# Loading an output projection with six consecutive rows per partition, and reordering attention's result to match

## The chip, the cores and the metric

The kernel runs on one core of one Trainium2 chip. The metric is the device time of one execution in microseconds (us); lower is better. The core has a matrix engine (TensorE, PE in the profile; its weight loads are PEld), a vector engine (VectorE, DVE), a scalar engine (ScalarE, ACT), GpSimd (POOL), a queue engine (SyncE, SP) and 16 DMA engines that move data from HBM into SBUF, the on-chip memory of 128 partitions. TensorE writes its results into PSUM.

## The reference

One token of 640 values passes through two kinds of layer, each applied twice: attention over a cached window (A), then a small mixer with an MLP (B). The weights and caches are the same both times.

```python
x = A_x
x = x + _A_ref(_layernorm(x), A_k_cache, A_v_cache, A_wq, A_wo)
x = x + _B_ref(_layernorm(x), B_w1, B_w2, B_w3, B_w4)
x = x + _A_ref(_layernorm(x), A_k_cache, A_v_cache, A_wq, A_wo)
x = x + _B_ref(_layernorm(x), B_w1, B_w2, B_w3, B_w4)

# _A_ref: 32 heads of 192, the last 4096 rows of each head's cache
q = (x @ wq).reshape(32, 192)
scores = q . k * 192 ** -0.5        # per head, over 4096 rows
o = softmax(scores) @ v             # per head, 192 values
return o.reshape(32 * 192) @ wo     # wo is 6144 x 640
```

All inputs are bfloat16. For a single token the shifts in `_B_ref` bring only zeros, so its `w1` and `w2` do not reach the result, and the kernel loads `w3` and `w4` alone.

## The kernel before, in words

**Groups.** The 32 heads are handled in 8 groups of 4 (`G = 4`). One `attention` call walks the groups in `order`: 0 to 7 in the first attention, 7 to 0 in the second. A head's K window is one tile of 128 partitions x 6144 bfloat16 values (1536 KB), 32 consecutive cache rows to a partition, so 12,288 consecutive bytes of HBM to each partition; V is the same. These tiles live in 15 `slots`, given out and taken back through the deque `free`. At the turn of the two attentions group 7 keeps its transposed K and its V in SBUF (`keep_T`, `keep`), and the `wo` tiles of groups 6 and 7 stay too.

**Loads.** All large loads are issued by SyncE, in the order of the list `plan` makes: for each group the K heads of the next group and the V heads of this one in turn, after the second V head the group's part of `wo` (L117), and at the end of an attention the mixer's `w3` and `w4` (`load_w34`). A load is issued when the program reaches it (`ahead`) and its slot is free. `plan` fixes 14 loads of `wo` in all: 8 in the first attention, 6 in the second (groups 5 to 0).

**One group.** `keys` transposes K in 32x32 blocks on VectorE (L300, two instructions a head); `kmm` multiplies with the queries (L340), which `qproj` has brought into the block form `Q8` (L288). `soft_a`, `soft_b` and `soft_c` make the softmax (L356 to L401). `pv_rows` multiplies with V (L447), gathering four heads in `O_ps`: afterwards 32 partitions belong to one head each by a pattern that the 0/1 matrix `ho` selects.

**The end of a group, `evac_rows`.** ScalarE (L478) and VectorE (L479) scale and add the two halves of `O_ps` into `O_sb`, 128 partitions x 192. Four products with `O_sb` as weights and columns of `ho` (L482, L484, L486, L488), all in float32, sum over partitions and turn the result: `OT_ps` has 128 partitions x 6, one column for each 128 consecutive entries of the group's 768 outputs. A copy casts it to `osb` (L491).

**The output projection, `outproj`.** The group's 768 rows of `wo` are in `wo_g`, 128 partitions x 6 x 640. Row `t * 128 + p` lies in partition `p` at index `t` ("(t p) n -> p t n" on L117), so that a partition takes six separate rows of 1280 bytes. 30 products of one column (L498) add `wo_g[:, t, :]` times column `t` of `osb` into `y_ps`.

The last group of an attention (`gz`) is treated apart: two of its heads go through `pv_rows` and `evac_rows`, the other two through `pv_cols` and `evac_cols`, which makes `osb` in the order of 128 consecutive entries directly.

The tile `half` (128 x 3072 bfloat16) holds the softmax's `E` and `ET`, `O_lo`, `O_sb` and one of two `PT` tiles during attention, and a part of `w4` during the mixer (L135, L136).

Of the kernel before, what the change touches and what calls it, by code (L numbers as in the profile page):

```python
# [8 lines left out]
BF16 = mybir.dt.bfloat16  # L9
F32 = mybir.dt.float32  # L10
U32 = mybir.dt.uint32
ACTF = mybir.ActivationFunctionType
ALU = mybir.AluOpType
AX = mybir.AxisListType
PSUM = bass.MemoryType.PSUM

P = 128
G = 4
# [7 lines left out]
def kernel(  # L26
# [64 lines left out]
    O_lo = half[:, 2 * NC_S:2 * NC_S + 2 * Dh].bitcast(F32)  # L91
    PT_h = half[:, 2 * NC_S + 4 * Dh:2 * NC_S + 4 * Dh + 4 * G * J]
    O_sb = half[:, 2 * NC_S + 2 * Dh:2 * NC_S + 4 * Dh].bitcast(F32)

    def slot():
        return free.popleft()
# [13 lines left out]

    wo_t = {}

    def load_wo(g):
        if g in wo_t:
            return
        t = wop.tile([P, NOC, D], BF16, name="wo_g")
        nc.sync.dma_start(t[:], A_wo[g * GD:(g + 1) * GD, :].rearrange("(t p) n -> p t n", p=P))  # L117
        wo_t[g] = t

    NKA = FREE // F  # L120
# [66 lines left out]
    for x in range(2):  # L187
# [6 lines left out]
    nc.vector.tensor_reduce(  # L194
        out=ho8[:], in_=ident[:].rearrange("p (tl i e) -> p tl i e", tl=4, e=2)[:, :, 0:G], op=ALU.add, axis=AX.X)
    nc.vector.tensor_reduce(out=ho[:], in_=ho8[:].rearrange("p tl i -> p i tl"), op=ALU.add, axis=AX.X)
    hs = const.tile([P, G], F32, name="hs")
    hs8 = const.tile([P, 8], F32, name="hs8")
    nc.vector.tensor_reduce(
# [72 lines left out]
    def qproj(g, xn_bf):  # L272
        qT_ps = psm.tile([P, NOC], F32, tag="psm", name="qT_ps")
        for tl in range(NOC):
            t = g * NOC + tl
            for kc in range(ND):
                nc.tensor.matmul(  # L277
                    qT_ps[:, tl:tl + 1], lhsT=wq_t[kc][:, t * P:(t + 1) * P], rhs=xn_bf[:, kc:kc + 1],
                    start=(kc == 0), stop=(kc == ND - 1))
        Xq = sm.tile([P, NOC, 4], BF16, name="Xq")  # L280
        nc.vector.tensor_tensor(  # L281
            out=Xq[:], in0=qT_ps[:, :].unsqueeze(2).broadcast_to([P, NOC, 4]),
            in1=maskq[:, :].unsqueeze(1).broadcast_to([P, NOC, 4]), op=ALU.mult)
        Qrep_ps = psm.tile([P, NOC * 4], F32, tag="psm", name="Qrep_ps")
        nc.tensor.matmul(Qrep_ps[:], lhsT=Lb[:].rearrange("p a i -> p (a i)"), rhs=Xq[:].rearrange("p t b -> p (t b)"), start=True, stop=True)
        Q8 = sm.tile([P, 2, 2 * NCOL, 8], BF16, name="Q8", tag=f"Q8_{nq[0] % 2}", bufs=1)
        nq[0] += 1
        nc.vector.tensor_tensor(  # L288
            out=Q8[:],
            in0=Qrep_ps[:, :].rearrange("p (x c) -> p x c", x=2).unsqueeze(3).broadcast_to([P, 2, 2 * NCOL, 8]),  # L290
            in1=blk8[:].unsqueeze(2).broadcast_to([P, 2, 2 * NCOL, 8]), op=ALU.mult)
        Q_t[g] = Q8

# [182 lines left out]
    def evac_rows(g):  # L476
        m01, O_ps = sx[g]["m01"], O_t[g]
        nc.scalar.activation(O_lo, O_ps[:, Dh:2 * Dh], ACTF.Identity, scale=m01[:, 1:2])  # L478
        nc.vector.scalar_tensor_tensor(  # L479
            out=O_sb, in0=O_ps[:, 0:Dh], scalar=m01[:, 0:1], in1=O_lo, op0=ALU.mult, op1=ALU.add)  # L480
        OT_ps = psm.tile([P, 2, 3], F32, tag="psm", name="OT_ps")
        nc.tensor.matmul(OT_ps[:, :, 0], lhsT=O_sb[:, 0:P], rhs=ho[:, 0:4:2], start=True, stop=True,  # L482
                         skip_group_check=True)
        nc.tensor.matmul(OT_ps[:, :, 2], lhsT=O_sb[:, TB:Dh], rhs=ho[:, 1:4:2], start=True, stop=True,  # L484
                         skip_group_check=True)
        nc.tensor.matmul(OT_ps[0:TB, :, 1], lhsT=O_sb[:, P:Dh], rhs=ho[:, 0:4:2], start=True, stop=True,  # L486
                         tile_position=(0, 0), skip_group_check=True)
        nc.tensor.matmul(OT_ps[TB:P, :, 1], lhsT=O_sb[:, 0:TB], rhs=ho[:, 1:4:2], start=True, stop=True,  # L488
                         tile_position=(0, TB), skip_group_check=True)
        osb = sm.tile([P, 2, 3], BF16, name="osb")  # L490
        nc.vector.tensor_copy(osb[:], OT_ps[:])  # L491
        osb_t[g] = osb

    def outproj(g, pr, y_ps, first, last):
        osb = osb_t[g]
# [9 lines left out]
    def attention(order, xT_cur, xT_new, keep, loads):  # L505
        n_loaded = [0]

        def need(upto):
            while n_loaded[0] < min(upto, len(loads)):
                what = loads[n_loaded[0]]  # L510
                n_loaded[0] += 1
                if what[0] == "wo":
                    load_wo(what[1])
                elif what[0] == "w34":
                    load_w34()
                else:
                    load(*what)

        where = {what: n for n, what in enumerate(loads)}
        ahead = lambda *what: need(where.get(what, -1) + 1)  # L520

        def keys(h, whole=True):
            if h not in T_t and h not in half_t:
                ahead("K", h)
                trans_begin(h)
            if whole and h in half_t:
                trans_end(h)

        tot_ps, rstd = ln_stats(xT_cur)
        xn_bf = sm.tile([P, ND], BF16, name="xn_bf")  # L530
        ln_apply(xn_bf, xT_cur, tot_ps, rstd)
        y_ps = psY.tile([P, ND], F32, name="y_ps")
        g0, g1 = order[0], order[1]
        warm = g0 * G in T_t
        qproj(g0, xn_bf)
        for i in range(G):
            keys(g0 * G + i)
            kmm(g0, i)
            if not warm and i == 0:
                qproj(g1, xn_bf)  # L540
        if warm:
            need(G + 1)
        soft_a(g0)
        soft_b(g0)
        if warm:
            keys(g1 * G, whole=False)
            qproj(g1, xn_bf)
        soft_c(g0, g1 * G)
        kept = lambda g, i: ("V", g * G + i) in keep
        for n, g in enumerate(order[:-1]):  # L550
            nxt = order[n + 1]
            ahead_h = order[n + 2] * G if n + 2 < len(order) else None
            for i in range(G):
                keys(nxt * G + i)
                kmm(nxt, i)
                if i == G - 1:
                    soft_a(nxt)
                    soft_b(nxt)
                    if ahead_h is not None:
                        keys(ahead_h, whole=False)  # L560
                ahead("V", g * G + i)
                if i == 1 and ahead_h is not None:
                    qproj(order[n + 2], xn_bf)
                if i == 0:
                    norm_rows(g)
                pv_rows(g, i, kept(g, i))
            ahead("wo", g)
            soft_c(nxt, ahead_h)
            evac_rows(g)
            if ahead_h is not None:  # L570
                outproj(g, 0, y_ps, n == 0, False)
                outproj(g, 1, y_ps, False, False)
        gz = order[-1]
        for i in range(2):
            ahead("V", gz * G + i)
            pv_rows(gz, i, kept(gz, i), n_heads=2)
        outproj(g, 0, y_ps, False, False)
        outproj(g, 1, y_ps, False, False)
        ahead("wo", gz)
        norm_rows(gz)  # L580
        ahead("V", gz * G + 2)
        pv_cols(gz, 2, kept(gz, 2))
        evac_rows(gz)
        outproj(gz, 0, y_ps, False, False)
        ahead("V", gz * G + 3)
        pv_cols(gz, 3, kept(gz, 3))
        evac_cols(gz, 1)
        outproj(gz, 1, y_ps, False, True)
        Oc_t.clear()
        need(len(loads))  # L590
        nc.vector.tensor_tensor(out=xT_new[:], in0=xT_cur[:], in1=y_ps[:], op=ALU.add)
# [35 lines left out]
    def plan(order, have):  # L627
        loads = [("K", order[0] * G + i) for i in range(G)]
        for n, g in enumerate(order):
            for i in range(G):  # L630
                if n + 1 < len(order):
                    loads.append(("K", order[n + 1] * G + i))
                loads.append(("V", g * G + i))
                if i == 1:
                    loads.append(("wo", g))
        loads.append(("w34",))
        return [w for w in loads if w not in have]
# [4 lines left out]
    keep_T = {gl * G + i for i in range(G)}  # L642
    keep = {("V", gl * G + i) for i in range(G)}
    x1 = const.tile([P, ND], F32, name="x1")
    attention(first, xT, x1, keep, plan(first, set()))
    x2 = const.tile([P, ND], F32, name="x2")
    mixer(x1, x2)
# [1 line left out]
        del wo_t[g]  # L649
    have = keep | {("K", h) for h in keep_T} | {("wo", g) for g in wo_t}  # L650
    keep_T = set()
    x3 = const.tile([P, ND], F32, name="x3")
    attention(second, x2, x3, set(), plan(second, have))
    x4 = const.tile([P, ND], F32, name="x4")
# [37 lines left out]
```

## Time and profile before

| | |
|---|---|
| time, median of 3 runs | 540.31 us (539.6 to 540.43) |
| the profiled execution's own time | 539.87 us |
| its span, first to last instruction | 537.6 us |
| moved by DMA | 218.76 MB in 33,830 packets, mean 407 GB/s |
| busy share of the span | PE 59%, PEld 29%, DVE 51%, ACT 7% |
| granted TensorE clock, mean | 0.681 of full speed |

The profile is one execution seen by the hardware profiler. A line of a group reads: source line, engine, operation, output <- inputs, shapes, count | busy us, mean ns of one | idle time of the engine just ahead of it and what ended that. The slice rows cut the span into 40 pieces of 13.44 us. The chain is followed back from the last instruction to what released each step. L12 is line 12 of the kernel.

### The profile page before, as it was taken

To read this page: it belongs to the slowest core of one execution; us is meant where nothing else is said; L and a number is where in the kernel's file an instruction comes from. 1 tells how busy PE (TensorE), PEld (TensorE's weight loads), DVE (VectorE), ACT (ScalarE), POOL (GpSimd) and SP (SyncE) were. 2 spreads that over 40 slices of the span, in tenths; PEclk is the share of its full clock that TensorE was granted. 3 is DMA by queue.
4 is the path that set the end of the run, shared out by engine and by line. 5 is a ranking of instruction groups with operands and counts; after the bars stand their busy time and mean duration, and the time that the engine had idled before them with its cause. 6 is when DMAs were issued, how large, how long until landed. Compare 5 with 4: busy or idle time off the path is not lost.

```text
span 537.6 us, 8273 instructions
## 1 busy us (share of the span) xinstructions
PE 319.4 (59%) x3675; PEld 157.1 (29%) x3675; DVE 273.3 (51%) x398; ACT 36.3 (7%) x113; POOL 2.1 (0%) x11
## 2 busy tenths in 40 slices
PE   1154746574755757446585676765765658464574
PEld 0011322141322314222155333342322414132254
DVE  4176564464645457263422377675736446464412
ACT  1001010010100001010011101010101001010011
POOL 1000000000000000000000000000000000000000
PEclk9997777665577655777555677878565766657765
DMA  8999999999999999999999899999999999999995
GB/s 345 430 424 411 423 428 415 425 410 425 421 420 423 413 424 413 425 424 413 424 405 344 324 386 427 423 414 424 414 423 425 411 425 416 425 426 409 424 406 192
DMA packets 33830, 218.76 MB, mean 407 GB/s; under 512 B 2692, under 2 KB 16516, under 8 KB 17796
## 3 DMA queue, kind: packets, MB, share of 16 engines
q1 hardware_dynamic: 33786, 218.25, 98.5%
q8 instruction: 28, 0.46, 0.3%
q14 instruction: 6, 0.05, 0.0%
q10 hardware_dynamic: 10, 0.00, 0.0%
HBM read 218.24 MB, written 0.00 MB: 406 GB/s over the span
## 4 chain that ended last, share of the span: by engine, by line
DMA 64%; DVE 18%; PE 15%; issue 2%; ACT 1%; SPq 1%; DVEq 0%
DMA slot<-in_A_k_cache_dram 50%; DMA slot<-in_A_v_cache_dram 14%; DVE slot L300 13%; PE S_ps L340 8%; DVE pm L356 1%; DVE half L378 1%; PE y2T_ps L621 1%; PE qT_ps L277 1%; PE hT_ps L604 1%; PE O_ps L447 1%; PE pmT_ps L360 1%; PE O_ps L421 1%; PE y_ps L498 1%; PE O_ps L432 1%; SPq L101 0%
## 5 line engine op out<-in xcount | busy, mean ns | idle before, releaser
L300 DVE STREAM_TRANSPOSE slot<-slot 128x1536 uint32<-128x1536 uint32 x120 | 206.8, 1756 | 89.9 <-DMA slot<-in_A_k_cache_dram 89.7
L340 PE MATMUL S_ps<-slot,Q 128*8 128x512 bf16 x768 | 173.2, 564 | 119.5 <-DVE slot L300 118.0
L340 PEld LDWEIGHTS <-Q 128*8 128x8 bf16 x768 | 45.0, 104 | 213.3 <-issue 203.4
L447 PE MATMUL O_ps<-slot,half 128*8 128x384 bf16 x512 | 60.9, 440 | 0.0
L447 PE MATMUL O_ps<-slot,PT 128*8 128x384 bf16 x448 | 48.1, 435 | 0.0
L356 DVE TENSOR_REDUCE pm<-S_ps 128x1 f32<-128x512 f32 x16 | 11.1, 692 | 42.8 <-PE S_ps L340 42.8
L370 ACT COPY nb_sb<-nb_ps 128x1 f32<-128x1 f32 x16 | 2.5, 159 | 429.7 <-PE nb_ps L368 429.7
L281 DVE TENSOR_TENSOR Xq<-qT_ps,maskq 128x24 bf16<-128x24 f32 x16 | 2.9, 180 | 52.0 <-PE qT_ps L277 52.0
L447 PEld LDWEIGHTS <-half 128*8 128x8 bf16 x512 | 19.6, 98 | 19.0 <-issue 16.2
L277 PE MATMUL qT_ps<-xn_bf,slot 128*128 128x1 bf16 x480 | 15.2, 164 | 14.1 <-DMA slot<-in_A_wq_dram 11.8
L447 PEld LDWEIGHTS <-PT 128*8 128x8 bf16 x448 | 15.3, 99 | 16.6 <-issue 14.6
L277 PEld LDWEIGHTS <-slot 128*128 128x128 bf16 x480 | 13.7, 98 | 21.7 <-DMA slot<-in_A_wq_dram 13.4
L482 PE MATMUL OT_ps<-ho,half 128*128 128x2 f32 x32 | 9.2, 356 | 17.0 <-DVE half L479 17.0
L498 PE MATMUL y_ps<-osb,wo_g 128*128 128x1 bf16 x480 | 15.6, 165 | 4.3 <-DVE osb L491 3.7
L498 PEld LDWEIGHTS <-wo_g 128*128 128x128 bf16 x480 | 15.6, 104 | 5.5 <-issue 3.9
L491 DVE CAST osb<-OT_ps 128x6 bf16<-128x6 f32 x16 | 2.6, 165 | 26.7 <-PE OT_ps L488 26.7
L360 PE MATMUL pmT_ps<-ident,pmh 128*4 128x128 f32 x16 | 5.0, 314 | 18.1 <-DVE pmh L358 18.1
L387 PE MATMUL Pp_ps<-half,identb 128*32 128x32 bf16 x256 | 6.7, 235 | 14.5 <-DVE half L378 14.5
L378 DVE STREAM_TRANSPOSE half<-half 128x512 bf16<-128x512 bf16 x16 | 11.1, 691 | 4.6 <-ACT half L372 4.6
L482 PEld LDWEIGHTS OT_ps<-ho,half 128*128 128x128 f32 x32 | 7.8, 304 | 18.2 <-DVE half L479 18.2
L387 PEld LDWEIGHTS <-identb 128*32 128x32 bf16 x256 | 5.7, 115 | 20.5 <-issue 20.0
L372 ACT ACTIVATE half<-S_ps,nb_sb 128x512 bf16<-128x512 f32 x16 | 11.0, 687 | 0.5
(116 smaller groups left out, 188.1 us busy)
## 6 DMA issues: line engine op xcount, KB each, us to landing
slot<-in_A_k_cache_dram SPq DMA_DIRECT2D x60, 1536.0 KB, 24.0
slot<-in_A_v_cache_dram SPq DMA_DIRECT2D x60, 1536.0 KB, 23.9
wo_g<-in_A_wo_dram SPq DMA_DIRECT2D x14, 960.0 KB, 28.5
slot<-in_A_wq_dram SPq DMA_DIRECT2D x5, 1536.0 KB, 13.1
slot<-in_B_w_dram SPq DMA_DIRECT2D x2, 1536.0 KB, 23.6
slot<-in_B_w_dram SPq DMA_DIRECT2D x2, 1120.0 KB, 19.6
half<-in_B_w_dram SPq DMA_DIRECT2D x2, 640.0 KB, 8.5
slot<-in_B_w_dram SPq DMA_DIRECT2D x2, 384.0 KB, 17.6
```

Of the source, the lines that this page charges most:

```text
L277: nc.tensor.matmul(qT_ps[:, tl:tl + 1], lhsT=wq_t[kc][:, t * P:(t + 1) * P], rhs=xn_bf[:, kc:kc + 1], start=(kc == 0), stop=(kc == ND - 1))
L300: nc.vector.transpose(T[:, hf * HALF:(hf + 1) * HALF].bitcast(U32).rearrange("p (f j k) -> p j f k", f=NFB, j=HJ, k=32), Kn[:, hf * HALF:( ...
L340: nc.tensor.matmul(S_ps[r:r + 8, :], lhsT=Q_t[g][:, x, par * NCOL + 2 * f + t, :], rhs=Tv[:, f, :, t], start=(x == 0 and n == 0), stop=(n ...
L356: nc.vector.tensor_reduce(out=pm[:], in_=S_t[g][:], op=ALU.max, axis=AX.X)
L360: nc.tensor.transpose(pmT_ps[0:G, :], pmh[:, 0:G], ident[:, :])
L372: nc.scalar.activation(out=E, in_=S_ps[:], func=ACTF.Exp, bias=nb_sb[:, 0:1], scale=scale, accum_out=lpart[:, 0:1])
L378: nc.vector.transpose(ET.rearrange("p (j r) -> p j r", r=32), E.rearrange("p (j k) -> p j k", k=32))
L387: nc.tensor.matmul(two, lhsT=identb[:, 32 * tl:32 * (tl + 1)], rhs=ETv[:, :, 0:2, m].rearrange("p (j e) x -> p x j e", e=2), start=True, s ...
L421: nc.tensor.matmul(O_ps[:, pr, ca:ca + 1], lhsT=V[:, j * Dh + oa:j * Dh + oa + P], rhs=col(j), start=(j == 0), stop=(j == J - 1))
L447: nc.tensor.matmul(O_t[g][r:r + 8, :], lhsT=PT[:, i, jj, :], rhs=V[:, jj * 2 * Dh:(jj + 1) * 2 * Dh], start=(i == 0 and jj < 4), stop=(i = ...
L482: nc.tensor.matmul(OT_ps[:, :, 0], lhsT=O_sb[:, 0:P], rhs=ho[:, 0:4:2], start=True, stop=True, skip_group_check=True)
L498: nc.tensor.matmul(y_ps[:, n:n + 1], lhsT=wo_t[g][:, 3 * pr + t, n * P:(n + 1) * P], rhs=osb[:, pr, t:t + 1], start=(first and t == 0 and ...
```

## The change

For 12 of the 14 loads of `wo`, row `6 * p + t` of the group goes to partition `p` at index `t`: each partition takes six consecutive rows, 7680 consecutive bytes. The two loads left as they were are those of the last group of each attention (7 in the first, 0 in the second), which `in_chunks` names; group 7 of the second attention uses the tile loaded in the first.

So `osb` must hold entry `6 * p + t` in partition `p`, column `t`. For groups that are not in `in_chunks`, `evac_rows` makes it with one float32 product: the weights `hoX` are the 0/1 columns of `ho`, each repeated 32 times, and `OX_ps` holds each head's 192 values in 32 partitions. A multiplication by the mask `m32` (one where partition p and index i agree modulo 32) and a sum over i pick six values in each partition. This runs 7 times in the first attention (groups 0 to 6) and 6 times in the second (6 to 1). The group in `in_chunks` keeps the four products: 3 times in all.

Two constants are made at the start (`hoX`, `m32`), and the two `Q8` tiles become regions of `half` that were unused during attention.

```diff
+    Q8_o = 2 * NC_S + 4 * Dh + 4 * G * J
+    Q8_n = 2 * 2 * NCOL * 8
+    Q8_two = [half[:, Q8_o + n * Q8_n:Q8_o + (n + 1) * Q8_n].rearrange("p (x c e) -> p x c e", x=2, e=8) for n in range(2)]
...
-        nc.sync.dma_start(t[:], A_wo[g * GD:(g + 1) * GD, :].rearrange("(t p) n -> p t n", p=P))
+        rows = "(t p) n -> p t n" if g in in_chunks else "(p t) n -> p t n"
+        nc.sync.dma_start(t[:], A_wo[g * GD:(g + 1) * GD, :].rearrange(rows, p=P))
...
+    hoX = const.tile([P, G, 32], F32, name="hoX")
+    nc.vector.tensor_copy(hoX[:], ho[:].unsqueeze(2).broadcast_to([P, G, 32]))
+    m32 = const.tile([P, 32], F32, name="m32")
+    nc.vector.tensor_reduce(
+        out=m32[:], in_=ident[:].rearrange("p (m i) -> p i m", i=32), op=ALU.add, axis=AX.X)
...
-        Q8 = sm.tile([P, 2, 2 * NCOL, 8], BF16, name="Q8", tag=f"Q8_{nq[0] % 2}", bufs=1)
+        Q8 = Q8_two[nq[0] % 2]
...
+        osb = sm.tile([P, 2, 3], BF16, name="osb")
+        osb_t[g] = osb
+        if g not in in_chunks:
+            OX_ps = psm.tile([P, Dh], F32, tag="psm", name="OX_ps")
+            nc.tensor.matmul(
+                OX_ps[:], lhsT=hoX[:].rearrange("p h i -> p (h i)"), rhs=O_sb, start=True, stop=True)
+            nc.vector.tensor_tensor(
+                out=O_lo.rearrange("p (t i) -> p t i", i=32), in0=OX_ps[:].rearrange("p (i t) -> p t i", t=NOC),
+                in1=m32[:].unsqueeze(1).broadcast_to([P, NOC, 32]), op=ALU.mult)
+            with nc.allow_low_precision(reason="each sum has one term that is not zero"):
+                nc.vector.tensor_reduce(
+                    out=osb[:].rearrange("p a b -> p (a b)"), in_=O_lo.rearrange("p (t i) -> p t i", i=32),
+                    op=ALU.add, axis=AX.X)
+            return
...
+    in_chunks.add(gl)
     attention(first, xT, x1, keep, plan(first, set()))
...
+    in_chunks.add(second[-1])
     attention(second, x2, x3, set(), plan(second, have))
```

More of the change, by code (lines that the diff above doesn't have):

```diff
@@ L111 @@
     wo_t = {}
+    in_chunks = set()
     def load_wo(g):
@@ L285, in qproj @@
         nc.tensor.matmul(Qrep_ps[:], lhsT=Lb[:].rearrange("p a i -> p (a i)"), rhs=Xq[:].rearrange("p t b -> p (t b)"), start=True, stop=True)
-        Q8 = sm.tile([P, 2, 2 * NCOL, 8], BF16, name="Q8", tag=f"Q8_{nq[0] % 2}", bufs=1)
+        Q8 = Q8_two[nq[0] % 2]
         nq[0] += 1
         nc.vector.tensor_tensor(
-            out=Q8[:],
+            out=Q8,
             in0=Qrep_ps[:, :].rearrange("p (x c) -> p x c", x=2).unsqueeze(3).broadcast_to([P, 2, 2 * NCOL, 8]),
@@ L489, in evac_rows @@
                          tile_position=(0, TB), skip_group_check=True)
-        osb = sm.tile([P, 2, 3], BF16, name="osb")
         nc.vector.tensor_copy(osb[:], OT_ps[:])
-        osb_t[g] = osb
     def outproj(g, pr, y_ps, first, last):
```

## The prediction

> **What bounds the kernel now.** I read the page's slice rows first, since they tell which stage waits for what.
>
> ```profile
> DMA  8999999999999999999999899999999999999995
> GB/s 345 430 424 411 423 428 415 425 410 425 421 420 423 413 424 413 425 424 413 424 405 344 324 386 427 423 414 424 414 423 425 411 425 416 425 426 409 424 406 192
> DMA packets 33830, 218.76 MB, mean 407 GB/s; under 512 B 2692, under 2 KB 16516, under 8 KB 17796
> ...
> DMA 64%; DVE 18%; PE 15%; issue 2%; ACT 1%; SPq 1%; DVEq 0%
> ```
>
> The DMA engines are busy in nearly every slice, and the chain of waits is mostly DMA. Within the even plateau the rate alternates: about 425 GB/s, and 409 to 416 in roughly every second or third slice. Packets under 2 KB are half of all packets, and 14 x 768 = 10,752 of them are the 1280-byte rows of `wo`. So the second view is the windows, 7 us each, laid where a group's `wo` arrives (the first, second, sixth and eleventh) and on neighbours with K and V alone; the last two columns are DMA share and GB/s:
>
> ```profile
> 49.00:56.00 7.00, 3.67 (x37) 1.58 (x38) 6.01 (x10) 0.58 (x1) 0.00 (x0) 0.50 1.02 397
> 42.00:49.00 7.00, 2.73 (x16) 0.99 (x15) 3.44 (x6) 0.94 (x3) 0.00 (x0) 0.91 1.01 422
> 56.00:63.00 7.00, 5.35 (x77) 2.40 (x72) 4.19 (x5) 0.00 (x0) 0.00 (x0) 0.86 1.01 427
> 80.00:87.00 7.00, 6.74 (x90) 3.02 (x89) 4.06 (x6) 0.00 (x0) 0.00 (x0) 0.62 1.04 405
> 87.00:94.00 7.00, 1.86 (x39) 0.91 (x36) 2.79 (x4) 0.00 (x0) 0.00 (x0) 0.86 1.02 429
> 210.50:217.50 7.00, 6.73 (x100) 3.52 (x101) 3.90 (x5) 0.00 (x0) 0.00 (x0) 0.68 1.04 404
> 217.50:224.50 7.00, 1.10 (x17) 0.27 (x6) 3.09 (x3) 0.00 (x0) 0.00 (x0) 0.81 1.01 425
> 203.00:210.00 7.00, 4.61 (x45) 3.19 (x46) 5.01 (x10) 1.85 (x5) 0.00 (x0) 0.50 1.01 428
> 419.00:426.00 7.00, 6.73 (x99) 3.42 (x97) 3.81 (x4) 0.00 (x0) 0.00 (x0) 0.70 1.03 401
> ```
>
> The engines are as busy with `wo` as without (1.02 to 1.04 against 1.01), yet move less: a mean of 401.8 GB/s against 426.2. Time goes with rows, not only with bytes. The third view is the compute around `evac_rows`, and who waits for K:
>
> ```profile
> DVE slot L300 <- DMA slot<-in_A_k_cache_dram: 89.7, 29, 7.6
> ...
> DVE osb L491 <- PE OT_ps L488: 26.7, 16, 3.5
> ```
>
> VectorE waits 29 times, 3.1 us at the mean, for a K tile to land. That idle time covers what is added to it within a group. Last, where the chain leaves DMA (start, us, what):
>
> ```profile
> 250.63 28.50 DMA slot<-in_A_v_cache_dram
> ...
> 350.23 21.48 DMA slot<-in_A_k_cache_dram
> ```
>
> The last V of the first attention lands at 279.1; from there to 350 the chain is compute (end of the attention, mixer, warm start of the second). The three slices of 344, 324 and 386 GB/s lie in that stretch: `w3` and `w4`, then loads held back by slots that compute has not freed.
>
> **The change, part by part.**
>
> *The 12 loads.* In a window with one `wo` load, 426.2 - 401.8 = 24.4 GB/s are missing; over 7 us that is 171 KB, or 0.40 us at 426 GB/s. The load is 0.983 MB, which at 426 GB/s takes 2.31 us; so it takes 2.71. Each of 16 engines carries 48 rows of it: 56.4 ns a row of 1280 bytes. A K row of 12,288 bytes takes 12,288 / (426.2 / 16) = 461.3 ns. A line through both has 9.3 ns a packet and 0.0368 ns a byte. A row of 7680 bytes is then 291.9 ns, eight to an engine 2.34 us: 0.37 us saved a load, 12 x 0.37 = **4.5 us**. Bounds: the weakest window pair (405 against 429 and 422) gives a deficit near 0.34 us, less the 0.03 that the 7680-byte rows keep, so 0.31 and 3.7 us in all; the strongest (397 against 424.5, its neighbours' mean) gives 0.45 us, or 5.4 in all if nothing is kept. A 7680-byte row is not in the trace. It lies between 3072 bytes and 12,288, and K's rows, consecutive from partition to partition as these will be, are the nearest.
>
> [...]
>
> *Is the saving on the path?* Seven of the loads lie in the first attention, where DMA has no gap, so its last V lands 7 x 0.37 = 2.6 us earlier, and the compute stretch that starts there (279 to 350) moves as a whole: the evacuation inside it, at 332, belongs to group 7 and keeps its four products. Five lie in the second attention after 350, where DMA again has no gap: 1.9 us more. The `w3`/`w4` loads and the tail are as before, only earlier. The profile's own time of 539.87 (2.3 above its span) becomes 535.4.
>
> *The product in `evac_rows`, 13 times.* Removed: four products, eight passes of PE, 1.32 us in the timeline (514.02 to 515.34). Added: one float32 product of 192 columns, which the trace doesn't have. Low bound: two passes like L482's, 2 x 0.356 = 0.71 us. High: two loads of 0.30 (L482's PEld) and two streams of 192 columns by L360's 314 ns for 128, 0.47 each, 1.55 us. I take 1.25, one load hidden behind the other stream. So PE is even, within 0.6 us an evacuation either way.
>
> *Mask and sum.* The cast of 0.165 us (L491) goes. The multiplication is like L479, 128x192 with PSUM as input: 0.38 us. The sum is between L471 (4 elements, 157 ns) and L356 (512, 692 ns): 0.36 us for 192. Net +0.57 us of VectorE an evacuation, 13 x 0.57 = 7.4 us. Queued behind are L469 to L473 and the next K's transposes; on PE the 30 products of `outproj` wait for `osb`, and behind them the next `kmm`. I cost this at nothing: in the even stages the transposes then wait for K anyway (89.7 us in all), and PE waits for the transposes (L340, 118.0 us). It is thinnest at 355 to 357, the first new evacuation of the second attention, where VectorE has work from 350 to 368; but it idles 3.86 us right after, before the K that lands at 371.7, and the loads issued meanwhile have some 21 us of queue ahead of them. For the group before last (514), PE has pv_rows (2.73 us) ahead of the products that need `osb`, then idles 0.63 us for V. If the cover were gone everywhere, it would cost 7.4 us.
>
> *With one answer.* Two more instructions at the start (rows L171 and L173: 0.23 and 0.28 us) end long before the first K lands at 25.86. `Q8` in `half`: SyncE's loads into `half` (L135, L136) already wait for later readers of it, and the second attention's first `Q8` comes after the mixer has read `w4`. SyncE issues the same DMAs in the same order; an issue took 0.38 us. Each of the five loads of `wq`, and K behind them, is untouched.
>
> **The rivals.** *Half of it is hidden.* If only one attention's loads count, because the slots free no earlier in the warm start or a landing is paced by something other than rows, the gain is 1.9 to 2.6 us: 537.7 to 538.4. Against it: the chain enters the compute stretch by a V landing and leaves it by a K landing. *Rows are not the cost.* If the 0.40 us belong to the transfer as such (its stride, or its turn between K and V), nothing is saved: 540.3. Against it: K and V follow one another with no such loss, and so would a transfer shaped like theirs. *The added compute comes onto the path.* One mechanism: `osb` later by 0.57 us holds PE ahead of `kmm` and VectorE ahead of the transposes, slots free later, and SyncE issues later. It decides once an added 0.57 us meets a group whose wait for K is under that, in most of the 13; then 7.4 - 4.5 = +2.9 us: 543.2. Against it stands the mean wait of 3.1 us; for it, that these waits are what the shorter DMA reduces, though by 0.37 us a group only.
>
> A smaller doubt widens the range: the page counts 28 instruction fetches at 0.3% of 16 engines' span, so about 0.9 us each on a single DMA engine, and a landing waits for the last engine. If the slightly shorter program moves one to or from that engine, an end shifts by some 0.9 us.
>
> **How the numbers follow.** Forecast, all 12 loads on the path: 540.31 - 4.5 = 535.8 us, chance 0.74. Half: 0.12. Rows are not the cost: 0.08. Compute on the path: 0.06. The forecast's own range is 540.31 - 5.4 = 534.9 to 540.31 - 3.7 = 536.6, and with 0.5 us of spread and half a fetch's shift below, 534.4; the upper end reaches through the half case, 538.4. Left out are 0.14 and the tails. About 0.2% (1.1 us) is what a measurement of this kernel can tell from no change: forecast and half give faster 0.86; same 0.08; slower 0.06.
>
> **What would show it.** Packets fall by 12 x 640 = 7680 to about 26,150, those under 2 KB by 9,216 to 7,300. Windows over a new `wo` load show about 424 GB/s. The `OX_ps` product takes 0.7 to 1.55 us in two passes, the mask and sum about 0.38 and 0.36 us. VectorE's wait for K falls by 5 to 12 us, and the last V of the first attention lands near 276.5. I am wrong if such a window still shows about 402 GB/s, if VectorE's waits for K vanish, or if a gap opens in the DMA row outside the three slices after 282.

## The result, and the profile after

The changed kernel takes 534.33 us (median of 4 runs, 534.11 to 534.53) against 539.99 us for the kernel before (median of 4 runs, 539.6 to 540.43): 5.66 us less, a ratio of 0.9895 (95% interval 0.9878 to 0.9912). Two repeats gave 534.11 (0.9903, 0.9886 to 0.9921) and 534.3 (0.9905, 0.9888 to 0.9921). The forecast was 535.8; the result lies 0.07 us below the low end of its range, 534.4. The profiled execution took 534.18 us with a span of 532.3.

The page of the changed kernel, the rows that answer to those shown before:

```profile
DMA  8999999999999999999999899999999999999995
GB/s 348 428 426 423 420 428 424 428 423 425 422 425 426 422 424 426 424 425 422 422 407 338 326 415 428 421 424 425 423 425 422 426 428 423 423 425 425 420 406 193
DMA packets 26151, 218.76 MB, mean 411 GB/s; under 512 B 2692, under 2 KB 7300, under 8 KB 10116
...
DMA 71%; PE 14%; DVE 12%; issue 1%; ACT 1%; SPq 0%; DVEq 0%
```

The plateau no longer alternates: 420 to 428 where every second or third slice had 409 to 416. Packets fell by 7679, those under 2 KB by 9216. Between the two ends only the stretch between the attentions (407, 338, 326, 415) still dips. The chain of waits holds more DMA (71% for 64) and less VectorE (12% for 18).

Windows of the changed kernel, 7 us each; one `wo` load of consecutive rows arrives in the first, third and fifth, only K and V in the second and fourth (last column GB/s):

```profile
49.00:56.00 7.00, 3.76 (x38) 1.49 (x39) 6.22 (x10) 0.58 (x1) 0.00 (x0) 0.56 1.02 428
42.00:49.00 7.00, 3.31 (x20) 1.04 (x16) 3.44 (x6) 0.94 (x3) 0.00 (x0) 1.00 0.99 420
208.00:215.00 7.00, 6.46 (x92) 3.52 (x92) 4.25 (x7) 0.00 (x0) 0.00 (x0) 0.59 1.02 425
215.00:222.00 7.00, 1.86 (x32) 0.75 (x30) 3.44 (x4) 0.00 (x0) 0.00 (x0) 0.89 1.01 428
414.50:421.50 7.00, 6.72 (x113) 3.67 (x114) 4.14 (x6) 0.00 (x0) 0.00 (x0) 0.71 1.01 425
```

The first window moved 397 GB/s before and 428 now. A `wo` load is no longer to be told from K and V by the rate, 425 to 428 against 420 and 428; one window more over a `wo` load, 80.5 to 87.5 us, has 417.

The groups of the new product, mask and sum (busy us, mean ns of one | idle before), and `outproj`'s products, which wait for the sum:

```profile
L496 PE MATMUL OX_ps<-half,hoX 128*128 128x192 f32 x26 | 13.1, 608 | 15.4 <-DVE half L490 15.4
L498 DVE TENSOR_TENSOR half<-OX_ps,m 128x192 f32<-128x192 f32 x13 | 4.6, 357 | 14.3 <-PE OX_ps L496 14.3
L502 DVE TENSOR_REDUCE osb<-half 128x6 bf16<-128x192 f32 x13 | 4.6, 353 | 0.4
...
L521 PE MATMUL y_ps<-osb,wo_g 128*128 128x1 bf16 x480 | 15.5, 165 | 10.5 <-DVE osb L502 9.2
```

and `outproj`'s products before:

```profile
L498 PE MATMUL y_ps<-osb,wo_g 128*128 128x1 bf16 x480 | 15.6, 165 | 4.3 <-DVE osb L491 3.7
```

Two passes of the product, overlapping, take 1.01 us in all (13.1 / 13). PE idles 10.5 us ahead of `outproj` where it was 4.3: the dearer VectorE path does hold PE, by some 6 us in sum. That none of it can be seen at the end is what `evac_only` shows below; VectorE still waits for K, by the waits:

```profile
DVE slot L311 <- DMA slot<-in_A_k_cache_dram: 80.1, 26, 6.3
```

The chain enters the compute stretch at 276.71 (248.22 + 28.49), where it was 279.13:

```profile
248.22 28.49 DMA slot<-in_A_v_cache_dram
```

So far this is the forecast. What it lacked shows in one line of each kernel: the second attention's first 48 products (`kmm` of group 7, whose K was kept), by the window they fill. The columns are us, PE, PEld, DVE, ACT and POOL busy, the granted clock, DMA share, GB/s. Before, and after:

```profile
298.49:304.24 5.75, 5.75 (x48) 1.77 (x48) 0.00 (x0) 0.00 (x0) 0.00 (x0) 0.55 0.53 180
```

```profile
295.94:300.72 4.78, 4.78 (x48) 1.61 (x48) 0.00 (x0) 0.00 (x0) 0.00 (x0) 0.68 0.49 149
```

The same products took 0.97 us less, at a granted clock of 0.68 instead of 0.55. In windows of half a microsecond the clock reads 0.50 or 1.00, but for the one in which it changes, here before and after:

```profile
303.50:304.00 0.50, 0.50 (x8) 0.13 (x2) 0.00 (x0) 0.00 (x0) 0.00 (x0) 0.79 0.92 393
```

```profile
299.00:299.50 0.50, 0.50 (x16) 0.21 (x12) 0.00 (x0) 0.00 (x0) 0.00 (x0) 0.97 0.00 0
```

So 0.55 over 5.75 us means that the clock opened (went from 0.5 to 1.0) 5.2 us after the start, 0.68 over 4.78 that it opened after 3.1. The products stand in the chain of both profiles (before, then after), in the stretch where compute alone sets the time:

```profile
298.49 5.77 PE S_ps L340 x40
```

```profile
295.94 4.80 PE S_ps L351 x42
```

The profiled gain of 5.69 us (539.87 - 534.18) splits so: the 48 products start 2.55 us earlier; they are 0.97 shorter; from their end to the span's end is 1.78 shorter (233.36 to 231.58); and the time outside the span is 0.39 shorter (2.27 to 1.88).

### The profile page after: what moved, and what is told of

Read it like the earlier page. It is cut to its first block, busy times and chain, and to the rows that moved or that the text cites. A ratio compares the mean times of both kernels' runs of the same rounds, so it can differ in the third digit from the quotient of the medians.

```text
span 532.3 us, 8132 instructions
## 1 busy us (share of the span) xinstructions
PE 316.7 (59%) x3597; PEld 151.1 (28%) x3597; DVE 280.6 (53%) x413; ACT 36.3 (7%) x113; POOL 2.1 (0%) x11
## 4 chain that ended last, share of the span: by engine, by line
DMA 71%; PE 14%; DVE 12%; issue 1%; ACT 1%; SPq 0%; DVEq 0%
DMA slot<-in_A_v_cache_dram 37%; DMA slot<-in_A_k_cache_dram 34%; DVE slot L311 8%; PE S_ps L351 7%; PE y_ps L521 1%; PE qT_ps L288 1%; PE O_ps L458 1%; PE O_ps L432 1%; PE O_ps L443 1%; PE hT_ps L627 1%; PE y2T_ps L644 1%; DVE pm L367 1%; DVE half L389 0%; SPq L104 0%; PE OX_ps L496 0%
## 5 line engine op out<-in xcount | busy, mean ns | idle before, releaser
L311 DVE STREAM_TRANSPOSE slot<-slot 128x1536 uint32<-128x1536 uint32 x120 | 206.8, 1755 | 80.1 <-DMA slot<-in_A_k_cache_dram 80.1
L351 PE MATMUL S_ps<-slot,half 128*8 128x512 bf16 x768 | 172.6, 565 | 113.7 <-DVE slot L311 112.0
L351 PEld LDWEIGHTS <-half 128*8 128x8 bf16 x768 | 46.6, 104 | 204.1 <-issue 194.2
L458 PE MATMUL O_ps<-slot,half 128*8 128x384 bf16 x512 | 58.9, 432 | 0.0
L458 PE MATMUL O_ps<-slot,PT 128*8 128x384 bf16 x448 | 51.0, 463 | 0.0
L458 PEld LDWEIGHTS <-half 128*8 128x8 bf16 x512 | 19.4, 97 | 18.3 <-issue 15.0
L496 PE MATMUL OX_ps<-half,hoX 128*128 128x192 f32 x26 | 13.1, 608 | 15.4 <-DVE half L490 15.4
L521 PE MATMUL y_ps<-osb,wo_g 128*128 128x1 bf16 x480 | 15.5, 165 | 10.5 <-DVE osb L502 9.2
L498 DVE TENSOR_TENSOR half<-OX_ps,m 128x192 f32<-128x192 f32 x13 | 4.6, 357 | 14.3 <-PE OX_ps L496 14.3
L379 PE MATMUL nb_ps<-ngm,hsT 4*128 4x1 f32 x32 | 8.1, 319 | 6.0 <-DVE ngm L373 6.0
L496 PEld LDWEIGHTS OX_ps<-half,hoX 128*128 128x128 f32 x26 | 6.5, 311 | 16.5 <-DVE half L490 16.5
```

Source lines behind the costliest of these rows:

```text
L311: nc.vector.transpose(T[:, hf * HALF:(hf + 1) * HALF].bitcast(U32).rearrange("p (f j k) -> p j f k", f=NFB, j=HJ, k=32), Kn[:, hf * HALF:( ...
L351: nc.tensor.matmul(S_ps[r:r + 8, :], lhsT=Q_t[g][:, x, par * NCOL + 2 * f + t, :], rhs=Tv[:, f, :, t], start=(x == 0 and n == 0), stop=(n ...
L379: nc.tensor.matmul(nb_ps[:], lhsT=hsT[0:G, :], rhs=sx[g]["ngm"][0:G, :], start=True, stop=True)
L458: nc.tensor.matmul(O_t[g][r:r + 8, :], lhsT=PT[:, i, jj, :], rhs=V[:, jj * 2 * Dh:(jj + 1) * 2 * Dh], start=(i == 0 and jj < 4), stop=(i = ...
L496: nc.tensor.matmul(OX_ps[:], lhsT=hoX[:].rearrange("p h i -> p (h i)"), rhs=O_sb, start=True, stop=True)
L521: nc.tensor.matmul(y_ps[:, n:n + 1], lhsT=wo_t[g][:, 3 * pr + t, n * P:(n + 1) * P], rhs=osb[:, pr, t:t + 1], start=(first and t == 0 and ...
```

## The experiments

Theory A: rows give 4.1 to 4.5 us, and the rest is where the clock opens in the warm start. Theory B: rows give all, 0.47 us a load. Theory C: the shorter product path gives the last 1 us. Each kernel ran beside the kernel before.

**One part alone.** `loads_only`, of the changed kernel:

```diff
-        if g not in in_chunks:
+        if False:
             OX_ps = ...
```

> Only the row order of the 12 loads; the four products are kept for every group, so each of the 12 groups is projected with its results in the old order (its output is not the reference's). Theory A (rows and clock): DMA saves 0.34 to 0.37 us a load, 4.1 to 4.5 us, and up to 1.0 us more comes only if the first 48 products of the second attention (L340 before, 5.75 us; after 4.78) find the TensorE clock opened: 534.5 to 535.9 us. Theory B (rows alone): 0.47 us a load, all of it here: 534.3 us whatever the clock does. Theory C (the shorter product path gives the last 1.0 us): 535.3 to 535.9.

Measured: 535.49 us (534.38 to 535.97), ratio 0.9917 (0.9903 to 0.993). Its slice row has no dips but the one between the attentions (406, 337, 322, 415):

```profile
GB/s 346 428 426 423 422 426 424 427 423 426 423 425 425 423 426 426 424 423 425 424 406 337 322 415 430 422 425 425 421 424 427 425 425 425 424 425 425 419 407 190
```

Two runs lie at 534.4, three at 535.5 to 536.0. The rows' gain is there without the new product; the spread of 1.6 us is not a matter of rows, against B. The median lies in A's range and in C's alike.

`evac_only`, of the changed kernel:

```diff
-        rows = "(t p) n -> p t n" if g in in_chunks else "(p t) n -> p t n"
+        rows = "(t p) n -> p t n"
```

> Only the new product, mask and sum; all loads keep six separate rows, so 12 groups are projected in the wrong order (output is not the reference's). Theory A: no row is longer, so the last V of the first attention lands at 279.1 as before, and the time is that of before within 0.3 us, unless the 48 products at the warm start find another clock (then up to 1.0 us less). Theory B: 540.0, no change. Theory C: 539.0, in every round. The forecast's third rival (compute on the path) would show as 541 or more.

Measured: 538.64 us (538.28 to 539.58), ratio 0.998 (0.997 to 0.9991): 1.2 us faster at the median, which at first spoke for C. But its profiled run took 539.42 with a span of 537.6, exactly that of before, its V landing at 279.1 and its 48 products 5.71 us long:

```profile
250.12 29.00 DMA slot<-in_A_v_cache_dram
```

```profile
298.47:304.18 5.71, 5.71 (x48) 1.82 (x48) 0.00 (x0) 0.00 (x0) 0.00 (x0) 0.55 0.52 174
```

Its spans, 536.5 to 537.8, lie within those of the kernel before (536.3 to 539.1 in the 90 runs beside these experiments), but low among them: the median is 536.9, against 537.2 in the 90 and 537.6 in the 15 that ran beside it. What differs clearly is the time outside the span, 1.74 to 1.95 us against 2.08 or more in each of the 90. The added work costs nothing that can be seen; whether it helps the span by some tenths, by way of the clock, these runs leave open.

**One attention alone.** `first_only` and `second_only`:

```diff
 # first_only
-    in_chunks.add(second[-1])
+    in_chunks.update(second[2:])
 # second_only
-    in_chunks.add(gl)
+    in_chunks.update(first)
...
-    in_chunks.add(second[-1])
+    in_chunks.difference_update(second[2:-1])
```

> Consecutive rows in the first attention's 7 loads only; the second attention's loads and products as before, but for group 6, whose tile is kept. Theory A: last V lands 2.4 us earlier than 279.1, and the end is 2.4 to 2.6 us earlier, or 3.4 to 3.6 if the warm start's 48 products run faster: 536.5 to 537.6. Theory B: 7 x 0.47 = 3.3 us, 536.7, with the landing itself 3.3 us earlier (275.8). Half-hidden rival of the forecast: nothing gained here, 540.

> Consecutive rows in the second attention's 5 loads only; the first attention as before. Theory A: 5 x 0.34 to 0.37 = 1.7 to 1.9 us, 538.1 to 538.3, warm start as before (last V at 279.1, 48 products 5.75 us). Theory B: 5 x 0.47 = 2.4 us, 537.6.

Measured: 536.14 us (535.9 to 536.85; ratio 0.9938, 0.9926 to 0.9951) and 536.99 us (536.63 to 537.11; 0.9949, 0.9937 to 0.9961). Windows of `first_only`, one over a load of consecutive rows and one over a load of separate rows in the second attention:

```profile
49.00:56.00 7.00, 3.99 (x42) 1.62 (x45) 6.24 (x8) 0.58 (x1) 0.00 (x0) 0.60 1.02 427
382.00:389.00 7.00, 7.00 (x76) 2.69 (x76) 3.83 (x4) 0.00 (x0) 0.00 (x0) 0.55 1.03 399
```

Both orders in one kernel, 427 and 399 GB/s. The two gains (3.7 and 2.8 us) add up to more than the whole change gives, as they would if each held a share that is not the rows'. `first_only` lies 0.4 us below A's low end (536.5) and `second_only` 1.1 us below A's 538.1; both expectations left out the part outside the span, and the second fixed the 48 products at 5.75 us, which took 5.03 in its profile.

**The warm start's clock.** All profiles side by side; start and length of the 48 products and the granted clock from windows like those above; "rest" is the time from their end to the span's end (us):

| kernel | start | length | clock | rest |
|---|---|---|---|---|
| before | 298.49 | 5.75 | 0.55 | 233.4 |
| before_again | 298.42 | 5.09 | 0.63 | 233.2 |
| evac_only | 298.47 | 5.71 | 0.55 | 233.4 |
| q8_only | 297.99 | 4.71 | 0.69 | 233.4 |
| consts_too | 298.21 | 4.62 | 0.71 | 233.5 |
| first_only | 295.75 | 5.08 | 0.63 | 233.5 |
| second_only | 298.37 | 5.03 | 0.64 | 231.5 |
| loads_only | 296.11 | 4.79 | 0.68 | 231.6 |
| after | 295.94 | 4.78 | 0.68 | 231.6 |
| after_again | 295.61 | 4.87 | 0.66 | 231.6 |
| after_third | 296.01 | 4.91 | 0.66 | 231.6 |

The start falls into two classes by the first attention's rows: 298.33 at the mean with separate rows, 295.88 with consecutive ones, 2.45 us for 7 loads. So does the rest, by the second attention's rows: 233.4 and 231.6, 1.8 us for 5 loads. That is 0.35 and 0.36 us a load, whichever product path the kernel has: evac_only has the new one with separate rows, loads_only the old one with consecutive rows. The length follows the clock: 4.62 to 5.75 us with separate rows in the first attention (consts_too and before at its two ends), 4.78 to 5.08 with consecutive ones.

`before_busy` and `after_busy` tried to open the clock early, with 11 idle products in the mixer's gaps (5 after the products with `w3`, 2 after those with `w4`, 3 after the layer norm's, 1 after `qproj`); one of the four calls:

```diff
+    def busy(n):
+        for _ in range(n):
+            nc.tensor.matmul(O_two[nO[0] % 2][:], lhsT=identb[:], rhs=PT_sm[:, 0:2 * Dh], start=True, stop=True,
+                             skip_group_check=True)
...
+        busy(5 if T_t else 0)
```

> The kernel before, with 11 idle products (128x384, into an accumulator that is overwritten later) in the gaps of the mixer between the attentions, so that TensorE is not idle ahead of the second attention's first 48 products. Theory A (the last 1 us of the change is where the granted clock happens to open): with the clock open earlier the 48 products take 3 to 4.5 us instead of 5.75, the times lose their spread of 1.5 us, and the median falls by 1 to 2.5 us: 537.4 to 538.9. Theory C (the shorter product path gives it): no effect of this kind, 539.8 plus up to 0.5 us where an idle product is in the way.

> The changed kernel with the same 11 idle products. Theory A: both kernels then have the same clock at the warm start, and differ by the rows alone: 4.1 to 4.5 us below before_busy, plus 0.3 us that lies outside the span. Theory B (0.47 us a load): 5.6 us below before_busy. Theory C: 5.2 to 5.6 us below it.

Measured: 540.16 us (538.79 to 541.73; ratio 1.0008, 0.9994 to 1.0022) and 534.81 us (533.86 to 535.5; 0.9912, 0.9895 to 0.9928). A miss: the 48 products in the profiles ran at 0.67 and 0.58, within the range of the kernels without idle products, and before_busy's times spread over 2.9 us. The difference, 5.35 us, is above A's sum (4.4 to 4.8) and within C's; with that spread it decides nothing.

`before_open` and `after_open` put 22 such products in a row on the path, just ahead of the 48:

```diff
         qproj(g0, xn_bf)
+        if warm:
+            busy(22)
```

> The kernel before with 22 idle products (128x384, 7 us at the half clock) in a row on TensorE just ahead of the second attention's first 48 products. They lie on the path and cost some 5 to 7 us, but the granted clock must be open when the 48 start, in every run: they take about 3 us instead of 4.7 to 5.75. Theory A (clock): 541.5 to 545, and the 1 us between its quick and slow runs at this place is gone.

> The changed kernel with the same 22 idle products. Theory A: with the clock alike at the warm start, it lies below before_open by the rows alone, 4.4 us of span (2.55 by the start of the 48 products, 1.85 after them), plus 0.3 us outside the span: 4.6 to 4.9 us. Theories B and C (a gain of 0.47 us a load, or 1 us from the product path): 5.5 us or more below before_open.

Now the clock is open in both, before_open first, then after_open:

```profile
303.37:306.72 3.35, 3.35 (x49) 1.27 (x48) 0.00 (x0) 0.00 (x0) 0.00 (x0) 1.00 0.34 59
```

```profile
300.58:303.91 3.33, 3.33 (x49) 1.25 (x48) 0.00 (x0) 0.00 (x0) 0.00 (x0) 1.00 0.35 64
```

At 1.00 the 48 products take 3.35 and 3.33 us, alike. The times are 542.16 (541.76 to 543.09; ratio 1.0054, 1.0039 to 1.0068) and 538.23 (537.35 to 538.72; 0.9975, 0.9964 to 0.9985): 3.9 us apart, 4.4 in the profiles' spans (540.0 and 535.6) and 3.65 in the medians of the spans (540.05 and 536.4). That is 0.7 less than A expected of the medians and 1.6 less than B or C. The spread stayed near 1.4 us: the 22 idle products themselves were 5.71 and 5.38 us long, and now carry the moment of the opening (their weight loads come 0.32 us apart at first, and at the end 0.17: the last 9 in 1.53 us in before_open, the last 11 in 1.84 in after_open). With the 48 products alike, no gain beyond the rows is left in the span. That puts out B, and C as a saving of its own; it does not put out that the new product path acts by way of the clock.

**The time outside the span.** `q8_only` is the kernel before with the tiles `Q8` in `half`; `consts_too` adds `hoX` and `m32`:

```diff
-        Q8 = sm.tile([P, 2, 2 * NCOL, 8], BF16, name="Q8", tag=f"Q8_{nq[0] % 2}", bufs=1)
+        Q8 = Q8_two[nq[0] % 2]
...
 # consts_too besides
+    nc.vector.tensor_copy(hoX[:], ho[:].unsqueeze(2).broadcast_to([P, G, 32]))
+    nc.vector.tensor_reduce(
+        out=m32[:], in_=ident[:].rearrange("p (m i) -> p i m", i=32), op=ALU.add, axis=AX.X)
```

> The kernel before with the two Q8 tiles moved into the region of half, and nothing else. All theories: the span as before (536.5 to 538.1 by the clock at the warm start). Open is the part of the time outside the span: 2.1 to 2.3 us before, 1.75 to 1.95 in four of the kernels that carry the change or a part of it. If the memory layout does that, it is 1.8 to 1.95 here and the time 0.3 us below before; if the code of the constants or the shorter program does it, 2.1 to 2.3.

> The kernel before with Q8 in half and the two constants hoX and m32 made at the start, which nothing reads; loads and products as before. The 0.3 us outside the span: if the two instructions at the start bring it, 1.75 to 1.95 here (2.17 with Q8 alone); if the product path or the loads bring it, 2.1 to 2.3. The span: 536.4 to 538.0, by the clock, in all theories.

> The kernel before once more, for a second profile and more times. Theory A: the profile's 48 products and its span go together: 4.7 to 4.9 us with a span of 536.4 to 536.9, or 5.7 us with 537.5 to 538.0; their end to the span's end is 233.4 us either way.

Measured: q8_only 538.91 us (538.72 to 540.27; ratio 0.9991, 0.9979 to 1.0003), outside 2.12 to 2.31 and once 2.82: the layout does not do it. consts_too 539.52 (538.15 to 540.54; 1.0001, 0.9991 to 1.0011), outside four times 1.84 to 1.86 and eight times 2.34 to 2.88: both, in one program. before_again 539.29 (538.87 to 540.73; 0.9996, 0.9986 to 1.0007), outside 2.09 to 2.34, once 3.13; its profile has a length between the two named (5.09) and a span of 536.7, so A's pairing held in its order and not in its two values. The 0.3 to 0.4 us outside the span belong to no part of the change that these runs tell apart. Their cause is open.

**Luck or place.** The length of the 48 products differs from run to run as if drawn by lot, and the span with it. A had expected the second round of the changed kernel to spread over 1 to 1.5 us like the kernel before; five of its six times lay within 0.5 us (533.9 to 534.38). Its span was 532.1 to 532.7 in nine of the first ten runs, a narrow draw near the quick end. `after_third` is unchanged; `after_late` delays the warm start, to see whether its place in time decides the draw:

```diff
+        if order[0] * G in T_t:
+            for _ in range(6):
+                nc.vector.memset(Pp_ps[:], 0.0)
```

> The changed kernel a third time. In its 10 runs so far the span was 532.1 to 532.7 nine times, near the quick end of what the opening of the clock allows (532.0 to 533.6, by the kernel before's 536.4 to 538.0 less 4.4). [...]

> The changed kernel with six clears of a PSUM tile (0.49 us each on VectorE) ahead of the second attention's layer norm, so that its first 48 products start about 2.4 us later, at the time from the span's start at which they start in the kernel before (298.4). [...]

after_third: spans 532.3, 532.5, 532.5, 533.2, the narrow draw again, twelve of fourteen in all. after_late: 538.04 us (537.3 to 538.66; ratio 0.9973, 0.9963 to 0.9982), spans 535.5 to 536.8 with a median of 536.2, and in its profile:

```profile
299.05:304.94 5.89, 5.88 (x48) 1.82 (x48) 0.00 (x0) 0.00 (x0) 0.00 (x0) 0.53 0.36 113
```

The start moved by 3.1 us, not the 2.4 expected; the median of the spans moved by 3.75 (from 532.45 over the fourteen), and the spans lie evenly over 1.3 us, where twelve of the fourteen lay within 0.6. Of the 3.75 us, 0.3 lies after the 48 products (a rest of 231.9 where the table has 231.6). With the start moved by VectorE alone the narrow draw is gone, which speaks for the place of the warm start.

The place alone does not decide it. loads_only starts its 48 products at 296.11, after_third at 296.01, and yet loads_only's spans were 532.5, 532.5, 533.5, 533.6 and 533.9: three of five outside the narrow draw, the median 1.0 us later. It differs from the changed kernel by its product path alone, but it also ran in another round: the kernel before had a median span of 537.6 beside it, 537.4 and 536.9 beside the changed kernel's repeats. So the new product path may have a part in the draw, and with evac_only's low spans that is C in another form; five and eleven runs do not settle it. What sets the moment at which the clock opens, no run here shows.

## Why the prediction was right and where it failed

**The 12 loads: right.** 0.37 us a load was forecast from the windows, 0.35 and 0.36 were measured, 4.25 us in all for 4.5. A row of 7680 bytes fits the line through 1280 and 12,288 bytes: 417 to 428 GB/s in four windows over a `wo` load (417 from 80.5 to 87.5 us, 425 to 428 in the three above), 424 forecast; windows of K and V alone have 420 to 429, so the line is not tested more finely. With rows of 1280 bytes the rate was lower: 397 to 405 GB/s in the kernel before, and in `first_only` 399 beside 427 with 7680.

**On the path: right, in both attentions.** The last V came 2.4 us earlier (2.6 forecast), the second part 1.8 us shorter (1.9).

**Product, mask and sum: right in the sum.** 1.01 us for the product instead of 1.25 (1.32 for the four it replaced); mask and sum 357 and 353 ns (0.38 and 0.36 us forecast). The cover held: VectorE's wait for K fell from 89.7 to 80.1 us and stayed above zero in 26 places. evac_only shows no cost.

**The step that failed** is "the compute stretch that starts there (279 to 350) moves as a whole". It moved and became shorter: its 48 first products took 4.78 us instead of 5.75 because the clock opened 3.1 instead of 5.2 us after their start. In these two profiles that is 0.97 us, partly by luck: the second profiles of the two kernels have 5.09 and 4.87, only 0.22 apart. In the medians of the spans it is about 0.5 (537.2 over 90 runs less 532.45 over 14 is 4.75, less 4.25 for the rows). The profile before showed the clock at 0.55 in that stretch, but I read its length as fixed. Why the changed kernel's clock so often opens early stays open.

A second term was mis-sized with it: the profile's "2.3 above its span" was kept as a constant and became 1.8 to 1.9. Its cause is open too. A range with both, up to 0.97 + 0.39 us below, would have held the time; the bound of 5.4 us that I gave the rows was no substitute, since the rows kept to 4.25.

Two slips of the sum come on top. The base of 540.31 was the median of three runs and stood high: four runs have 539.99, the 90 runs of later rounds 539.55. So 0.3 to 0.8 us of the 1.47 between forecast and result is the base. And the low end takes off too little by its own words: 534.9 less 0.5 us of spread and less half a fetch's shift, 0.45, is 533.95, and 534.4 has only the spread in it. The wider end would have held the time, but by luck: neither allowance names the clock or the time outside the span, and no run here shows a shift by a fetch (the pages of both kernels count 28 instruction fetches at 0.3%).

Around the 48 products the clock has two levels in both kernels' profiles, 0.50 and 1.00 in the half-microsecond windows. The moment of its opening, worked out from the clock as above, ranged from 2.7 us after the start in consts_too (0.71 over 4.62 us) to 5.5 in after_late (0.53 over 5.89). Whether twelve narrow draws of fourteen are more than luck, no run here shows.

**The rivals.** Half hidden: out, by the table's starts and rests, 2.45 us for the first attention's loads and 1.8 for the second's. Rows not the cost: out as a forecast, since the loads did get shorter; but the new order has fewer packets and no stride at once, and no run here tells one from the other. Compute on the path: out, by evac_only.

## What to carry to other kernels

Where the DMA engines are busy throughout and the rate still dips, divide the missing bytes by the packets in the dip: here some 9 ns a packet, an estimate from rows of 1280 and 12,288 bytes. A weight load in longer rows gave back 0.35 to 0.36 of the 0.40 us that were missing, and can do so if the other operand can be brought to the same order behind a wait that is already there. A stretch of compute on the path need not simply move when what precedes it gets shorter (its 48 products took 4.78 us here where they had taken 5.75): look at the granted clock at its start, and carry the difference between the clock's early and late opening (here 4.6 to 5.9 us for 48 products) in the range. For gains under one per cent, compare spans and times separately, over runs enough to see early and late openings, and take the base from as many.

## What was not expected of the hardware

- The same 48 products took 3.3 us at a granted clock of 1.00, 4.6 us at 0.71 and 5.9 us at 0.53, with no other compute engine busy in those windows.
- Eleven idle products in the mixer's gaps did not open the clock ahead of the 48 (0.67 over 4.82 us in before_busy, so that it opened 3.2 us after their start, though PE was busy some 5.7 us of the 6 from 290 to 296); 22 in a row did (1.00 over the 48).
- The time outside the span has levels that mostly stay with a program: 1.74 to 1.95 us in evac_only, 2.08 or more in all 90 runs of the kernel before; consts_too has two (1.85 and 2.34 or more).
